# A fourth fold for the odd columns of an FFT done by matrix multiplication, and inverse tiles run one ahead

## Chip, cores, metric

One core of one Trainium2 chip. The metric is device time in microseconds (us) of one execution. TensorE (PE in the profile) multiplies, VectorE (DVE) and ScalarE (ACT) do elementwise work and copies, GpSimd (POOL) here mostly issues stores. The "granted clock" is the share of TensorE's full clock that the profile shows as granted, 1.00 being all of it. A run is "fast" when it is not over 1.5% above the fastest run of the same kernel; all comparisons below are between fast runs, except where a single look is named as such.

## The reference, cut to what matters

```python
def f(A_x, A_w_r, A_w_i, B_w1, B_b1, B_w2, B_b2, gate_w, B_x):      # S=2048, D=1024, F=3584, bf16
    x = A_x
    g = sigmoid((x * gate_w).sum(-1, keepdims=True))
    a = irfft2(rfft2(x) * (w_r + 1j * w_i))                         # spectral branch
    b = relu(B_x @ w1 + b1)**2 @ w2 + b2                            # MLP branch
    return g * a + (1 - g) * b
out, vjp = jax.vjp(f, ...);  return (out, *vjp(grad_out))           # forward and all gradients
```

## The kernel before

The transforms along D = 1024 and part of S are matmuls with small constant tables in fp16. Symmetry of cosine and sine is used by "folds": VectorE forms sums and differences of an entry and its mirror image, which halves the tables. A tile of 128 rows passes a row stage (eight matmuls of 128 columns into PSUM tile `pk`, copied by ScalarE to `ft`) and a column stage (eight matmuls into `pu`: four for the even columns, four for the odd). There are 16 forward tiles of x, 16 forward tiles of the gradient, and 32 inverse tiles. Names: P = 128, Q = 256, H = 512; T = 0 is x, T = 1 the gradient; `V` is VectorE's tensor_tensor; `fps` is a PSUM pool in which row and column stages share two buffers.

```python
def first_columns(fb, cf, T, i, ft, earlier=None):                   # forward
    pu = fps.tile([P, 2, H], FP32, name="pu", tag="ps2", bufs=2)
    column_stage(FWD, pu, ft, cf, earlier)
    u = fb.tile([P, D], FDT, name="u", tag="u", bufs=2)
    nc.scalar.copy(out=u[:].rearrange("p (h b r) -> p b h r", h=2, b=2),
                   in_=pu[:].rearrange("p b (h r) -> p b h r", h=2))
    st(out=z_scr[T]..., in_=u[:])

FWD = (  # (bank, first column, columns, skip, start/stop)
    (0, 0, 2*P, 0, 1), (0, 0, P+1, 0, 2), (0, 2*P, P, 0, 3), (0, 3*P, P, 0, 3),     # even
    (1, 0, 2*P, P, 1), (1, 0, 2*P, P, 2), (1, P, 2*P, P, 1), (1, P, 2*P, P, 2),     # odd: 4 x 256
)

# inverse, for each T and tile i:
    r = ...; ld(out=r, in_=y_scr...)
    pk = ...; eight matmuls (128 columns) from r;  rt = ...; nc.scalar.copy(out=rt[:], in_=pk[:])
    yield                                     # other work's matmuls are put in here
    pu = ...; column_stage(INV, pu, rt, ci)   # the same tile's
    nc.scalar.copy(out=e[:], in_=pu[:])
    ...                                       # VectorE: ev, tt, yo; store
    yield 2

# the first ~100 us, in program order (cut):
for i0 in range(0, NT, 4):
    gate(i0)                                  # scales four dbn tiles, VectorE
    next(stage, None)                         # stage: row or column stage of the next x tile
    for k in (i0 // 2, i0 // 2 + 1):
        turned(dbT, k, ..., nc.vector.tensor_copy)   # PE transposes into pt, VectorE copies to dbT
        next(stage, None)
    for k in (i0 // 2 + 2, i0 // 2 + 3):
        x_pair(k)                             # PE transposes, ScalarE copies to xT
        next(stage, None)
    ...
```

## Time and profile before

| | before |
|---|---|
| time, median of 4 runs (lowest to highest) | 1342.63 us (1342.42 to 1343.85) |
| PE busy | 98% of 1340.5 us |
| forward stages of x beside the first MLP matmuls | up to about 100 us |
| forward stages of the gradient | from 134 us, in a stretch (134 to 352 us) with PE busy for 216.79 of 218 us |
| inverse stages | 815 to 924 us (x), 924 to 1141 us (gradient) |

The page's busy shares, the three slices of the first 100 us and the rows of the column stages are in the prediction below. Columns: length, then busy us (count) of PE, weight loads, DVE, ACT, POOL, granted clock, DMA share, GB/s.

```profile
15.00:85.00 70.00, 65.49 (x711) 45.57 (x719) 67.61 (x143) 53.94 (x107) 13.93 (x21) 1.00 0.59 201
```
VectorE is busy for 67.61 of 70 us, 97%: more than PE, which has 4.5 us free here. And of PE's waits in the first 134 us (instruction, what it waits for: us in total, times, longest), this one will grow:

```profile
PE pt L543 <- DVE dbT L544: 2.0, 3, 1.0
```

### The profile page before, as it was taken

How to read it: one execution, taken by the hardware profiler on the slowest of the kernel's cores; microseconds unless marked ns; L12 is line 12 of the kernel's file. 1: busy time of each engine (PE TensorE's matmuls, PEld its weight loads, DVE VectorE, ACT ScalarE, POOL GpSimd, SP SyncE). 2: the span in 40 equal slices, each digit the busy share in tenths (PEclk: the TensorE clock that was granted, in tenths of full speed). 3: DMA queues.
4: the chain of work that ended last, by engine and by line, in shares of the span. 5: the costliest groups of instructions: out<-in, count | busy, mean ns of one | idle time of the engine just before them, and what ended most of it. 6: DMA issues, size and time to landing. Idle time of an engine off the chain costs nothing. (4 is left out here: it accounts for less than half of the span.)

```text
span 1340.5 us, 18698 instructions
## 1 busy us (share of the span) xinstructions
PE 1311.1 (98%) x6974; PEld 638.2 (48%) x7082; DVE 802.1 (60%) x1541; ACT 419.9 (31%) x658; POOL 295.7 (22%) x484
## 2 busy tenths in 40 slices
PE   7999999999999999999999999999999999999998
PEld 5654444444444444444444445455444444444443
DVE  7966767666665695677666772233655676742232
ACT  6854555555433323332333333343101111000000
POOL 0222223222222343434432222111000000000000
PEclk9999999999999999999999999999999999999999
DMA  8558778787778988888877558677878854753530
GB/s 285 186 178 253 253 235 258 241 254 236 215 236 247 270 248 188 222 177 230 222 179 181 128 164 265 216 229 231 207 194 225 253 168 134 210 166 95 151 103 24
DMA packets 217093, 273.30 MB, mean 204 GB/s; under 512 B 16989, under 2 KB 152171, under 8 KB 217003
## 3 DMA queue, kind: packets, MB, share of 16 engines
q1 hardware_dynamic: 181306, 153.84, 43.5%
q0 software_dynamic: 35696, 118.27, 27.3%
q8 instruction: 55, 0.90, 0.3%
q14 instruction: 36, 0.29, 0.1%
HBM read 147.25 MB, written 118.51 MB: 198 GB/s over the span
## 5 line engine op out<-in xcount | busy, mean ns | idle before, releaser
L619 PE MATMUL ph<-xT,w1g 128*128 128x512 bf16 x866 | 214.5, 381 | 2.9 <-ACT rT L621 1.2
L629 PE MATMUL pd<-dbT,w2T 128*128 128x512 bf16 x879 | 210.6, 379 | 2.5 <-DVE w2T L651 0.7
L840 PE MATMUL pw<-grd,res 128*128 128x512 bf16 x896 | 201.7, 379 | 0.0
L823 PE MATMUL pw<-dbn,grp 128*128 128x512 bf16 x875 | 199.9, 379 | 1.2 <-issue 0.2
L906 PE MATMUL acc<-w,hblk 128*128 128x512 bf16 x874 | 196.3, 379 | 1.2
L948 PE MATMUL accg<-w1Tr,hblk 128*128 128x512 bf16 x878 | 192.8, 379 | 0.9
L948 PEld LDWEIGHTS <-hblk 128*128 128x128 bf16 x896 | 87.6, 98 | 106.1 <-issue 0.9
L629 PEld LDWEIGHTS <-w2T 128*128 128x128 bf16 x896 | 87.3, 98 | 104.6 <-issue 1.4
L823 PEld LDWEIGHTS <-grp 128*128 128x128 bf16 x896 | 86.8, 98 | 103.0 <-issue 0.9
L906 PEld LDWEIGHTS <-hblk 128*128 128x128 bf16 x896 | 87.1, 98 | 99.4
L619 PEld LDWEIGHTS <-w1g 128*128 128x128 bf16 x896 | 87.0, 98 | 99.2 <-issue 2.8
L840 PEld LDWEIGHTS <-res 128*128 128x128 bf16 x896 | 86.5, 98 | 99.3 <-issue 1.1
L621 ACT ACTIVATE rT<-ph,b1col 128x512 bf16<-128x512 f32 x112 | 77.0, 687 | 144.9 <-PE ph L619 135.1
L633 DVE SCALAR_TENSOR_TENSOR dhT<-pd,rT 128x512 bf16<-128x512 f32 x112 | 75.2, 671 | 65.4 <-PE pd L629 57.3
L953 DVE TENSOR_TENSOR gxo<-accg,g 128x512 bf16<-128x512 f32 x32 | 22.1, 691 | 107.0 <-PE accg L948 103.5
L738 DVE STREAM_TRANSPOSE stg<-h2T 128x512 int32<-128x512 int32 x56 | 39.8, 711 | 73.7 <-ACT h2T L622 73.7
L827 ACT CAST wo<-pw 128x512 bf16<-128x512 f32 x56 | 32.8, 585 | 143.1 <-PE pw L823 132.2
L835 POOL DMA_DIRECT2D out_dram<-wo x112 | 56.0, 506 | 92.1 <-ACT wo L827 75.4
L498 DVE TENSOR_TENSOR ev<-e 128x256 f16<-128x256 f16 x32 | 9.2, 289 | 111.4 <-ACT e L495 111.4
L845 ACT CAST wo<-pw 128x512 bf16<-128x512 f32 x56 | 32.8, 587 | 127.2 <-PE pw L840 117.6
L490 ACT CAST rt<-pki 128x1024 f16<-128x1024 f32 x32 | 32.4, 1014 | 126.2 <-PE pki L488 126.0
L622 ACT ACTIVATE h2T<-rT 128x512 bf16<-128x512 bf16 x112 | 70.6, 630 | 3.1
(174 smaller groups left out, 1509.8 us busy)
## 6 DMA issues: line engine op xcount, KB each, us to landing
h2T_scr<-h2T POOLq DMA_DIRECT2D x28, 512.0 KB, 4.3
h_scr<-stg POOLq DMA_DIRECT2D x28, 512.0 KB, 6.9
dhT_scr<-dhT POOLq DMA_DIRECT2D x28, 512.0 KB, 8.0
dh_scr<-stgd POOLq DMA_DIRECT2D x28, 512.0 KB, 6.9
grp<-h_scr SPq DMA_DIRECT2D x112, 128.0 KB
grd<-dh_scr SPq DMA_DIRECT2D x112, 128.0 KB
hblk<-h2T_scr SPq DMA_DIRECT2D x8, 1792.0 KB
hblk<-dhT_scr SPq DMA_DIRECT2D x8, 1792.0 KB
```

Of the source, the lines that this page charges most:

```text
L619: mm(ph[:], lhsT=w1g[:, dc, fc % 2 * P : (fc % 2 + 1) * P], rhs=xT[:, dc, ss], start=(dc == 0), stop=(dc == DC - 1))
L621: nc.scalar.activation(rT[:], ph[:], ACT.Relu, bias=b1col[:, fc : fc + 1])
L622: nc.scalar.activation(h2T, rT[:], ACT.Square)
L629: mm(pd[:], lhsT=w_[:, ec // 2, ec % 2 :: 2], rhs=dbT[:, ec, ss], start=(ec == 0), stop=(ec == DC - 1),)
L633: return STT(out=dhT, in0=pd[:], scalar=2.0, in1=rT[:], op0=ALU.mult, op1=ALU.mult, accum_out=gb1part[:, fc, sb : sb + 1],)
L738: nc.vector.transpose(out=stg[:, :, c, :], in_=h2T[:, c, :].bitcast(I32).rearrange("p (b i) -> p b i", i=32))
L823: mm(pw[:], lhsT=cur[:, t // 2, 2 * fb_ * P + t % 2 : 2 * (fb_ + 1) * P : 2], rhs=dbn[:, t, hf * H : (hf + 1) * H], start=(t == 0), stop=( ...
L827: last = nc.scalar.copy(out=wo[:, hf * H : (hf + 1) * H], in_=pw[:])
L835: st(out=dst[q], in_=wo[32 * q : 32 * (q + 1), :])
L840: mm(pw[:], lhsT=xr[t][:, d_ * P : (d_ + 1) * P], rhs=cur[:, t], start=(t == 0), stop=(t == NT - 1),)
L906: mm(acc[:], lhsT=cur[:, fc, t2::2], rhs=w2[:, fc, cs], start=(fc == 0), stop=(fc == FC - 1))
L948: mm(acc[:], lhsT=cur[:, fc, t2::2], rhs=w1T[:, fc, 2 * hf : 2 * hf + 2, :], start=(fc == 0), stop=(fc == FC - 1),)
```

## The change

Intent: the odd columns have one more symmetry, between column l and D/2 - l. If sums and differences of such pairs are formed, each of the odd bank's four matmuls needs 128 columns in place of 256. In the forward stage VectorE forms them after the matmuls (from a new tile `w`), in the inverse before them (tile `rf`). Second, the inverse loop is reordered so that the rows of tile n are issued before the columns of tile n-1. The core of the diff (constant tables, row order and unchanged lines of the inverse cut):

```diff
     def first_columns(fb, cf, T, i, ft, earlier=None):
-        column_stage(FWD, pu, ft, cf, earlier)
+        column_stage(pu, ft, cf, earlier)
         u = fb.tile([P, D], FDT, name="u", tag="u", bufs=2)
-        nc.scalar.copy(out=u[:].rearrange("p (h b r) -> p b h r", h=2, b=2), in_=pu[:].rearrange(...))
+        w = fb.tile([P, 2, 2, 2, P // 2], FDT, name="w", tag="w", bufs=2)
+        nc.scalar.copy(out=w[:].rearrange("p c x g i -> p (c x g i)"), in_=pu[:, 1, :])
+        nc.scalar.copy(out=u[:].rearrange("p (h b r) -> p b h r", h=2, b=2)[:, 0], in_=pu[:, 0, :]...)
+        X, Y = (w[:, :, x].rearrange("p c g i -> p g c i") for x in range(2))
+        V(out=uv[:, 1::2, :, 0 : P // 2], in0=X, in1=Y, op=ALU.add)
+        V(out=uv[:, 3::-2, :, P - 1 : P // 2 - 1 : -1], in0=X, in1=Y, op=ALU.subtract)
...
-        (1, 0, 2 * P, P, 1), (1, 0, 2 * P, P, 2), (1, P, 2 * P, P, 1), (1, P, 2 * P, P, 2),
+        (1, 0, P, 3), (1, P, P, 3), (1, 2 * P, P, 3), (1, 3 * P, P, 3),
...
+        def folded(n):
+            fold[n] = fb.tile([P, 2, 2, P], FDT, name="rf", tag="rf", bufs=2)
+            rv = r[n][:].rearrange("p (c l) -> p c l", c=2)
+            a, b = rv[:, :, 1:Q:2], rv[:, :, H - 1 : Q : -2]
+            V(out=fold[n][:, 0], in0=a, in1=b, op=ALU.add)
+            V(out=fold[n][:, 1], in0=a, in1=b, op=ALU.subtract)
...
-            nc.scalar.copy(out=e[:], in_=pu[:])
+            nc.scalar.copy(out=e[:, 0, :], in_=pu[:, 0, :])
+            nc.scalar.copy(out=e[:, 1, :]..., in_=pu[:, 1, :]...)
...
+        load(0), load(1)
+        folded(0)
+        for n in range(len(tiles) + 1):
+            if n < len(tiles):
+                rows_back(n)
+                yield
+            if n > 0:
+                columns_back(n - 1)
+            if n + 2 < len(tiles):
+                load(n + 2)
+            if n + 1 < len(tiles):
+                folded(n + 1)
+            yield
```

More of the change, by code (lines that the diff above doesn't have):

```diff
@@ L65, in build_consts @@
     l4, l42 = np.arange(0, D // 2 + 1, 4), np.arange(2, D // 2, 4)
-    lo = np.concatenate([np.arange(1, D // 2, 4), np.arange(3, D // 2, 4)])
-    d0, d1 = np.arange(P), np.arange(P, 2 * P)
-    dz, dh = d0.copy(), d0.copy()
-    dz[0], dh[0] = Q, P
+    lo = np.concatenate([np.arange(1, Q, 4), np.arange(3, Q, 4)])
+    d0, dO = np.arange(P), np.arange(1, Q, 2)
+    dh, dz = d0.copy(), 2 * d0
+    dh[0], dz[0] = P, Q
     blk_n = np.concatenate([np.zeros((P, P + 1)), -np.sin(w(l4[1:-1], d0))], axis=1)
@@ L73, in build_consts @@
         blk_n, np.cos(w(l4, d0)), np.cos(w(l42, d0)), -np.sin(w(l42, dh)),
-        np.cos(w(lo, d0)), np.cos(w(lo, d1)), -np.sin(w(lo, dz)), -np.sin(w(lo, d1)),
+        np.cos(w(lo, 2 * d0)), np.cos(w(lo, dO)), -np.sin(w(lo, dO)), -np.sin(w(lo, dz)),
     ]
@@ L79, in build_consts @@
     cof = lambda l: np.where((l == 0) | (l == 2 * Q), 1.0, 2.0)[:, None]
-    dq = np.arange(Q)
-    dzq = dq.copy()
-    dzq[0] = Q
     m4, m42 = np.arange(0, D // 2, 4), np.arange(2, D // 2, 4)
-    m1, m3 = np.arange(1, D // 2, 4), np.arange(3, D // 2, 4)
+    mo = np.arange(1, Q, 2)
     da = np.arange(P + 1)
@@ L90, in build_consts @@
         ev, cof(m4) * np.cos(v(m4, da)), 2.0 * np.cos(v(m42, d0)), -2.0 * np.sin(v(m42, dh)),
-        2.0 * np.cos(v(m1, dq)), 2.0 * np.cos(v(m3, dq)), -2.0 * np.sin(v(m1, dzq)), -2.0 * np.sin(v(m3, dzq)),
+        2.0 * np.cos(v(mo, 2 * d0)), 2.0 * np.cos(v(mo, dO)), -2.0 * np.sin(v(mo, dz)), -2.0 * np.sin(v(mo, dO)),
     ]
@@ L249, in row_stage @@
         pk = fps.tile([P, 8, P], FP32, name="pk", tag="ps2", bufs=2)
-        for b, (row, o) in enumerate(((5, P), (4, 0), (4, P), (5, 0), (3, 0), (3, P), (1, 0), (1, P))):
-            first_ = mm(pk[:, b, :], lhsT=f[:, row, o : o + P], rhs=kmat, start=True, stop=True)
+        even = [(row, slice(o, o + P)) for row, o in ((5, P), (4, 0), (4, P), (5, 0))]
+        odd = [(row, slice(o, Q, 2)) for row, o in ((3, 0), (3, 1), (1, 1), (1, 0))]
+        for b, (row, o) in enumerate(even + odd):
+            first_ = mm(pk[:, b, :], lhsT=f[:, row, o], rhs=kmat, start=True, stop=True)
             if b == 0:
@@ L259, in first_columns, with column_stage @@
         pu = fps.tile([P, 2, H], FP32, name="pu", tag="ps2", bufs=2)
-        column_stage(FWD, pu, ft, cf, earlier)
+        column_stage(pu, ft, cf, earlier)
         u = fb.tile([P, D], FDT, name="u", tag="u", bufs=2)
+        w = fb.tile([P, 2, 2, 2, P // 2], FDT, name="w", tag="w", bufs=2)
+        nc.scalar.copy(out=w[:].rearrange("p c x g i -> p (c x g i)"), in_=pu[:, 1, :])
         nc.scalar.copy(
-            out=u[:].rearrange("p (h b r) -> p b h r", h=2, b=2), in_=pu[:].rearrange("p b (h r) -> p b h r", h=2)
+            out=u[:].rearrange("p (h b r) -> p b h r", h=2, b=2)[:, 0], in_=pu[:, 0, :].rearrange("p (h r) -> p h r", h=2)
         )
+        uv = u[:].rearrange("p (g c i) -> p g c i", g=4, c=2)
+        X, Y = (w[:, :, x].rearrange("p c g i -> p g c i") for x in range(2))
+        V(out=uv[:, 1::2, :, 0 : P // 2], in0=X, in1=Y, op=ALU.add)
+        V(out=uv[:, 3::-2, :, P - 1 : P // 2 - 1 : -1], in0=X, in1=Y, op=ALU.subtract)
         st(out=z_scr[T][:].rearrange("c (p i) l -> i (c p) l", i=S2)[i], in_=u[:])
-    FWD = (
-        (0, 0, 2 * P, 0, 1), (0, 0, P + 1, 0, 2), (0, 2 * P, P, 0, 3), (0, 3 * P, P, 0, 3),
-        (1, 0, 2 * P, P, 1), (1, 0, 2 * P, P, 2), (1, P, 2 * P, P, 1), (1, P, 2 * P, P, 2),
-    )
-    INV = FWD[:4] + ((1, 0, Q, 0, 1), (1, 0, Q, 0, 2), (1, Q, Q, 0, 1), (1, Q, Q, 0, 2))
-    def column_stage(table, pu, ft, mat, earlier=None):
+    BLOCKS = (
+        (0, 0, 2 * P, 1), (0, 0, P + 1, 2), (0, 2 * P, P, 3), (0, 3 * P, P, 3),
+        (1, 0, P, 3), (1, P, P, 3), (1, 2 * P, P, 3), (1, 3 * P, P, 3),
+    )
+    def column_stage(pu, ft, mat, earlier=None):
         o = 0
-        for b, (bank, lo, n, skip, f_) in enumerate(table):
-            out = pu[:, bank, lo : lo + n]
-            if skip:
-                out = pu[:, bank, :].rearrange("p (h c i) -> p c h i", h=2, c=2)[:, lo // P]
+        for b, (bank, lo, n, f_) in enumerate(BLOCKS):
             first_ = mm(
-                out, lhsT=ft[:, b, :], rhs=mat[:, o : o + n],
+                pu[:, bank, lo : lo + n], lhsT=ft[:, b, :], rhs=mat[:, o : o + n],
                 start=bool(f_ & 1), stop=bool(f_ & 2), skip_group_check=True,
@@ L480, in fft_out @@
         ld(out=ci[:], in_=cten["ci"].ap())
-        for T in range(2):
-            for i in range(NT):
-                r = fb.tile([P, H, 2], FDT, name="r", tag="r", bufs=3)
-                ld(out=r[:].rearrange("p j b -> p (j b)"), in_=y_scr[T][:].rearrange("c (p i) l -> i (c p) l", i=S2)[i])
-                pk = fps.tile([P, 8, P], FP32, name="pki", tag="ps2", bufs=2)
-                rf = r[:].rearrange("p j b -> p (j b)")
-                for b, (im, l_) in enumerate(((1, 0), (0, 0), (0, 2), (1, 2), (0, 1), (0, 3), (1, 1), (1, 3))):
-                    mm(pk[:, b, :], lhsT=rf[:, im * H + l_ : (im + 1) * H : 4], rhs=ki[:], start=True, stop=True)
-                rt = fb.tile([P, 8, P], FDT, name="rt", tag="rt", bufs=2)
-                nc.scalar.copy(out=rt[:], in_=pk[:])
-                yield
-                pu = fps.tile([P, 2, H], FP32, name="pui", tag="ps2", bufs=2)
-                column_stage(INV, pu, rt, ci)
-                e = fb.tile([P, 2, H], FDT, name="e", tag="e", bufs=2)
-                nc.scalar.copy(out=e[:], in_=pu[:])
-                ev = fb.tile([P, 2, Q], FDT, name="ev", tag="ev", bufs=2)
-                A, B = (e[:, 0, o : o + Q].rearrange("p (c d) -> p c d", c=2) for o in (0, Q))
-                V(out=ev[:, :, 0:P], in0=A, in1=B, op=ALU.add)
-                evf = ev[:].rearrange("p c d -> p (c d)")
-                V(out=evf[:, Q:P:-1], in0=A[:, 0, :], in1=B[:, 0, :], op=ALU.subtract)
-                V(out=evf[:, 2 * Q - 1 : Q + P : -1], in0=B[:, 1, 1:], in1=A[:, 1, 1:], op=ALU.subtract)
-                nc.vector.tensor_copy(out=ev[:, :, P : P + 1], in_=e[:, 0, P::Q].rearrange("p (c o) -> p c o", o=1))
-                tt = fb.tile([P, 2, 2, Q], FDT, name="tt", tag="tt", bufs=2)
-                V(out=tt[:, 0].rearrange("p a b -> p (a b)"), in0=evf, in1=e[:, 1, :], op=ALU.add)
-                V(out=tt[:, 1].rearrange("p a b -> p (a b)"), in0=evf, in1=e[:, 1, :], op=ALU.subtract)
-                yo = fb.tile([P, D], FDT, name="yo", tag="yo", bufs=2)
-                yv = yo[:].rearrange("p (a l) -> p a l", a=2)
-                V(out=yv[:, :, 0:Q], in0=tt[:, :, 0, :], in1=tt[:, :, 1, :], op=ALU.add)
-                V(out=yv[:, ::-1, H - 1 : Q : -1], in0=tt[:, :, 0, 1:Q], in1=tt[:, :, 1, 1:Q], op=ALU.subtract)
-                nc.vector.tensor_copy(out=yo[:, 0::Q], in_=tt[:, :, :, 0].rearrange("p a b -> p (a b)"))
-                st(out=ax_scr[T][i][:], in_=yo[:])
-                if T == 0 and i % 2 == 1:
-                    fc = 2 * (i - 1)
-                    if fc < FC:
-                        ld(out=w2[:, fc : fc + 4, :], in_=B_w2[fc * P : (fc + 4) * P, :].rearrange("(q p) e -> p q e", p=P))
-                yield 2
@@ new lines, in fft_out, with load @@
+        tiles = [(T, i) for T in range(2) for i in range(NT)]
+        r, fold, rt = {}, {}, {}
+        def load(n):
+            T, i = tiles[n]
+            r[n] = fb.tile([P, D], FDT, name="r", tag="r", bufs=3)
+            ld(out=r[n][:], in_=y_scr[T][:].rearrange("c (p i) l -> i (c p) l", i=S2)[i])
+        def folded(n):
[4 more added lines that the diff above has]
+            V(out=fold[n][:, 1], in0=a, in1=b, op=ALU.subtract)
@@ new lines, in rows_back @@
+        def rows_back(n):
+            pk = fps.tile([P, 8, P], FP32, name="pki", tag="ps2", bufs=2)
+            even = [r[n][:, im * H + l_ : (im + 1) * H : 4] for im, l_ in ((1, 0), (0, 0), (0, 2), (1, 2))]
+            odd = [fold[n][:, sign, im] for sign, im in ((0, 0), (1, 0), (1, 1), (0, 1))]
+            for b, block in enumerate(even + odd):
+                mm(pk[:, b, :], lhsT=block, rhs=ki[:], start=True, stop=True)
+            rt[n] = fb.tile([P, 8, P], FDT, name="rt", tag="rt", bufs=2)
+            nc.scalar.copy(out=rt[n][:], in_=pk[:])
@@ new lines, in columns_back @@
+        def columns_back(n):
+            T, i = tiles[n]
+            pu = fps.tile([P, 2, H], FP32, name="pui", tag="ps2", bufs=2)
+            column_stage(pu, rt[n], ci)
+            e = fb.tile([P, 2, H], FDT, name="e", tag="e", bufs=2)
+            nc.scalar.copy(out=e[:, 0, :], in_=pu[:, 0, :])
+            nc.scalar.copy(
+                out=e[:, 1, :].rearrange("p (c d x) -> p c d x", c=2, x=2),
+                in_=pu[:, 1, :].rearrange("p (c x d) -> p c d x", c=2, x=2),
+            )
+            ev = fb.tile([P, 2, Q], FDT, name="ev", tag="ev", bufs=2)
+            A, B = (e[:, 0, o : o + Q].rearrange("p (c d) -> p c d", c=2) for o in (0, Q))
+            V(out=ev[:, :, 0:P], in0=A, in1=B, op=ALU.add)
+            evf = ev[:].rearrange("p c d -> p (c d)")
+            V(out=evf[:, Q:P:-1], in0=A[:, 0, :], in1=B[:, 0, :], op=ALU.subtract)
+            V(out=evf[:, 2 * Q - 1 : Q + P : -1], in0=B[:, 1, 1:], in1=A[:, 1, 1:], op=ALU.subtract)
+            nc.vector.tensor_copy(out=ev[:, :, P : P + 1], in_=e[:, 0, P::Q].rearrange("p (c o) -> p c o", o=1))
+            tt = fb.tile([P, 2, 2, Q], FDT, name="tt", tag="tt", bufs=2)
+            V(out=tt[:, 0].rearrange("p a b -> p (a b)"), in0=evf, in1=e[:, 1, :], op=ALU.add)
+            V(out=tt[:, 1].rearrange("p a b -> p (a b)"), in0=evf, in1=e[:, 1, :], op=ALU.subtract)
+            yo = fb.tile([P, D], FDT, name="yo", tag="yo", bufs=2)
+            yv = yo[:].rearrange("p (a l) -> p a l", a=2)
+            V(out=yv[:, :, 0:Q], in0=tt[:, :, 0, :], in1=tt[:, :, 1, :], op=ALU.add)
+            V(out=yv[:, ::-1, H - 1 : Q : -1], in0=tt[:, :, 0, 1:Q], in1=tt[:, :, 1, 1:Q], op=ALU.subtract)
+            nc.vector.tensor_copy(out=yo[:, 0::Q], in_=tt[:, :, :, 0].rearrange("p a b -> p (a b)"))
+            st(out=ax_scr[T][i][:], in_=yo[:])
+            if T == 0 and i % 2 == 1:
+                fc = 2 * (i - 1)
+                if fc < FC:
+                    ld(out=w2[:, fc : fc + 4, :], in_=B_w2[fc * P : (fc + 4) * P, :].rearrange("(q p) e -> p q e", p=P))
```

## The prediction

Its sum came to -14.2 + 3 - 2.5 = -13.7 us, 1328.9 us. Rival 1 is the records of 98 ns: a gain of 4 x (112.5 - 98) x 64 = 3.7 us, about 1339 us, and 0.68 us for a column stage. The 162 ns are 2 x 587 - 1012 ns, the 0.3 us of signalling is what the 1.32 us of the example leave beside the copy of 1.01 us, and the 1 to 1.5 us for an eviction are an estimate of that size.

> **What bounds the kernel now.** I read the page's busy shares and slices first, then the busy time by stretch, then the groups by shape, then the timeline of the matrix engine around the two column stages, and last which waits hold that engine.
>
> From the page (busy us, share of the span; below it busy tenths in 40 slices of 33.5 us):
> ```profile
> PE 1311.1 (98%) x6974; PEld 638.2 (48%) x7082; DVE 802.1 (60%) x1541; ACT 419.9 (31%) x658; POOL 295.7 (22%) x484
> ...
> PE   7999999999999999999999999999999999999998
> ...
> DVE  7966767666665695677666772233655676742232
> ```
> TensorE (PE) is busy in nearly the whole span of 1340.5 us and the granted clock is full in every slice, so a microsecond of matmul taken out should be a microsecond off the end, except where something else already decides PE's pace. The only slice in which VectorE (DVE) also shows 9 is the second one. The stretches of the span (length, PE, weight loads, DVE, ACT, POOL busy, clock, DMA share, GB/s) say the same in microseconds:
> ```profile
> 0.00:33.50 33.50, 26.01 (x280) 18.68 (x284) 24.23 (x63) 22.99 (x47) 2.01 (x7) 1.00 0.82 285
> 33.50:67.00 33.50, 32.50 (x358) 23.02 (x362) 31.72 (x64) 27.49 (x52) 7.28 (x11) 1.00 0.56 187
> 67.00:100.00 33.00, 30.36 (x228) 16.97 (x229) 22.72 (x49) 18.62 (x33) 8.12 (x13) 1.00 0.52 179
> ```
> Those first 100 us are where the forward stages of x run: DVE has only 1.8 us free between 33.5 and 67 us. From 815 us to 924 us, where the first half of the inverse stages runs, DVE is busy for 33.6 of 109 us, and ACT for 45.0: plenty of room.
>
> A busy figure of PE is not its throughput, because one record lasts longer than the distance to the next one. So for the price of the column stage I use distances between starts in the timeline (start us, duration of the merged run, engine, line, what, count):
> ```profile
> 896.15 0.91 PE L281 MATMUL pui<-ci,rt 128*128 128x256 f16 x8
> 896.89 1.89 PE L840 MATMUL pw<-grd,res 128*128 128x512 bf16 x8
> 898.62 0.61 PE L488 MATMUL pki<-ki,r 128*128 128x128 f16 x8
> 899.07 3.62 PE L840 MATMUL pw<-grd,res 128*128 128x512 bf16 x16
> ```
> The eight matmuls of one inverse column stage take 896.89 - 896.15 = 0.74 us; the eight of a row stage, each of 128 columns, 899.07 - 898.62 = 0.45 us, or 56 ns each; the eight of 512 columns between them 1.73 us, or 216 ns each. Between those two a matmul costs (216 - 56)/(512 - 128) = 0.417 ns a column and about 3 ns, which makes 109 ns for 256 columns; single records in the column stages start 112 to 113 ns apart.
>
> [...]the row stage loads weights for each of its matmuls and still starts one every 56 ns, although a load's own record lasts 98 to 113 ns. [...](424 ns for 510 elements with a reversed operand, 424 ns for 512 without, both below); no tensor_tensor of fp16 with step 2 runs in the kernel before, and the new inverse fold has one. [...]the trace's copies of 512 columns (587 ns) and of 1024 (1012 ns) leave 162 ns.
>
> The rows (busy us, mean ns; idle us before them and its releasers):
> ```profile
> L281 PE MATMUL pu<-cf,ft 128*128 128x256 f16 x160 | 28.5, 274 | 0.1
> L281 PE MATMUL pui<-ci,rt 128*128 128x256 f16 x160 | 28.5, 274 | 4.5 <-ACT rt L490 3.8
> ...
> L845 ACT CAST wo<-pw 128x512 bf16<-128x512 f32 x56 | 32.8, 587 | 127.2 <-PE pw L840 117.6 <-issue 4.8 <-DMA out_dram<-wo 4.7
> L495 ACT CAST e<-pui 128x1024 f16<-128x1024 f32 x32 | 32.4, 1012 | 73.6 <-DVE ot L907 40.3 <-PE pui L281 27.2 <-issue 5.2
> ...
> L508 DVE TENSOR_TENSOR yo<-tt 128x512 f16<-128x512 f16 x32 | 13.6, 424 | 7.5 <-DMA ax_scr<-yo 6.9
> L509 DVE TENSOR_TENSOR yo<-tt 128x510 f16<-128x510 f16 x32 | 13.6, 424 | 0.0
> ...
> L498 DVE TENSOR_TENSOR ev<-e 128x256 f16<-128x256 f16 x32 | 9.2, 289 | 111.4 <-ACT e L495 111.4
> ```
>
> **The change, part by part.**
>
> *Removed from PE.* There are 32 forward and 32 inverse column stages. In each the odd bank's four matmuls go from 256 to 128 columns; their count, the even bank's four and all row stages keep their sizes. 4 x (112.5 - 57) = 222 ns per stage, so 64 x 0.222 = 14.2 us. All of it lies on the engine that sets the end. The new column stage should take about 0.74 - 0.22 = 0.52 us. This alone is 1.06% of 1342.6.
>
> *Added to DVE, forward.* Two tensor_tensor of 256 fp16 elements a tile. Records of this size last 289 ns and follow each other at some 0.20 us in the timeline; the new ones have inner runs of 64 with step 1 or -1, so I take 0.20 to 0.3 us. For the 16 tiles of x, 16 x 2 x 0.2 to 0.3 = 6.4 to 9.6 us come into the first 100 us. About a third of them fall into the stretch with 1.8 us of DVE to spare, so 1 to 2 us of it must push out what PE waits for (dbT, w2T, the folds). Elsewhere in the stage [...]PE waits for it now and then. I charge 3 us as a loss, a judgement; PE itself gives back 16 x 0.222 = 3.6 us there. So the early part is about even. The 16 tiles of the gradient run in the stretch from 134 us, where DVE has a third of the time free: no charge.
>
> *Added to DVE, inverse.* Two tensor_tensor of 256 elements with step 2, [...]in stretches where it is not the bound. No charge by itself.
>
> *Split of the PSUM copy.* One ACT copy of 1024 columns becomes two of 512: 2 x 587 - 1012 = 162 ns more, 64 x 0.162 = 10.4 us of ACT, on an engine with 69% free. It holds the PSUM pair 0.16 us longer.
>
> *Moved: one tile ahead.* Before, the column stage of a tile needs the copy of its own row stage. In the order of instructions the two stand only 5 to 7 long matmuls (1.1 to 1.5 us) apart in many places, and next to each other twice in the last part, while the copy takes 1.0 us and some 0.3 us of signalling. Example:
> ```profile
> 1028.34 0.61 PE L488 MATMUL pki<-ki,r 128*128 128x128 f16 x8
> 1030.11 0.91 PE L281 MATMUL pui<-ci,rt 128*128 128x256 f16 x8 [1.16 <-ACT rt L490]
> ```
> 1.77 us from start to start instead of 0.45: 1.32 us lost. Taking in every inverse column stage the start distance in front of it less the cost of the matmul there, 17 of 32 have such a hole, 7.2 us in sum (the row's 4.5 us of idle leaves out the draining end of the record before). In the changed kernel the row copy has a whole row stage's distance, so most of these go. But in the built order the new kernel also has places where row and column stages of two or three tiles stand close together (twice in the last part, thrice in the first), and they share two PSUM buffers, so some must wait for an eviction: 1 to 1.5 us each. I give 4.7 us of new holes: a net gain of 2.5 us.
>
> *Transfers.* Both constant tables shrink from 1665 to 1153 columns; not on the path. The w2 loads come one tile later, but the last one was issued 32 us before its first use. Still hidden.
>
> Sum: -14.2 + 3 - 2.5 = -13.7 us, 1328.9.
>
> **Rivals.**
> 1. *Weight loads take over:* a 128-column matmul cannot go below its load. [...]at 98 ns 3.7 us[...]. For: [...]the 98 ns records. Against: the row stage's 56 ns, even with its strided loads of 113 ns. Unlikely.
> 2. *DVE and ACT become the bound in the first 100 us:* all 10 us of new DVE work turn into PE waits. Then 1336. For: slice two. Against: slices one, three and four, with a third free.
> 3. *PSUM ping-pong:* bunched stages and the longer eviction cost more than the run-ahead saves, say 5 us net: 1336. For: two buffers only, and ACT's copies in the last part already wait for DVE (40.3 us "<-DVE ot"). Against: most stages of the new order alternate strictly, one between each 16 or 28 long matmuls.
> 4. *The holes nearly all go and the early part loses nothing:* 1342.6 - 14.2 - 7.2, about 1321.
>
> **Range and chances.** Rivals 2 to 4 give the edges: 1321 to 1336. Faster by over 2% needs under 1315.8, 27 us, more than all matmul savings plus all holes (21.4 us): 3%. Slower by over 2% needs PE to wait 40 us more: 1%.
>
> **What would show each step.** The distance from start to start over a column stage: 0.52 us (right), 0.6 or more (rival 1). The busy time by stretch before 100 us: the x stages should end at about the same time as before; 5 us later is rival 2. The waits for "rt" should vanish and holes at inverse stages sum to some 5 us; over 10 is rival 3. [...]The prediction is wrong if the early part reorders itself into something quite different, because a third of all PE idle lies there and the instruction order in it changes most.

## The result, and the profile after

The changed kernel takes 1337.7 us (median of 4 fast runs, 1336.4 to 1338.12), against 1342.63 us before. The ratio is 0.996, 95% interval 0.9942 to 0.9977; here and below a ratio is the mean time of one kernel's fast runs over that of the other's of the same rounds, so it isn't quite the ratio of the medians. A gain of 0.4%: within 2%, as expected, but 8.8 us slower than the 1328.9 us foretold and above the upper end of the range, 1336.

The page of the changed kernel (busy us; slices in tenths):

```profile
PE 1298.0 (97%) x6974; PEld 630.2 (47%) x7082; DVE 836.0 (63%) x1669; ACT 424.5 (32%) x722; POOL 295.7 (22%) x484
...
PE   7889999999999999999999999999999899999998
...
DVE  6986777676666596785667863434756776842232
```
PE's busy time fell by 13 us, but the span by only 5.9 us (1340.5 to 1334.6 in the profiled runs). The second and third digits of PE went from 9 to 8. The same three stretches as in the prediction show it for the changed kernel, and after them stands the window from 15 to 85 us:

```profile
0.00:33.50 33.50, 23.87 (x238) 16.81 (x241) 22.31 (x58) 20.97 (x42) 1.47 (x6) 1.00 0.80 274
33.50:67.00 33.50, 29.90 (x370) 21.77 (x373) 32.47 (x78) 28.99 (x58) 7.21 (x11) 1.00 0.56 186
67.00:100.00 33.00, 28.02 (x231) 16.12 (x234) 26.62 (x65) 20.08 (x46) 7.93 (x12) 0.95 0.48 162
```
```profile
15.00:85.00 70.00, 59.42 (x666) 41.23 (x673) 66.41 (x155) 53.12 (x112) 12.13 (x19) 0.98 0.57 195
```
From 15 to 85 us PE is busy for 6 us less and has also *done* less (666 matmul records against 711), while VectorE is nearly as full as before (66.41 us, 95%).

To place the 5.9 us I cut both traces at the same points of the work, by the first weight load of a stage; below, this table is called the ledger. "x" reaches from the first MLP matmul's load to the 129th load of that kind.

| stretch | before | after | difference | foretold |
|---|---|---|---|---|
| start, to the first MLP matmul | 9.13 | 9.66 | +0.5 | 0 |
| x: forward stages of x | 104.02 | 108.84 | +4.8 | -0.6 |
| forward stages of the gradient | 350.68 | 347.74 | -2.9 | -3.6 |
| weight gradients, spectral middle | 353.68 | 352.88 | -0.8 | 0 |
| inverse, first half | 106.44 | 101.80 | -4.6 | } -9.6 |
| inverse, second half | 217.06 | 213.75 | -3.3 | } |
| rest | 199.49 | 199.97 | +0.5 | 0 |
| sum | 1340.5 | 1334.6 | -5.9 | -13.7 |

(The foretold column divides the prediction's -14.2 of matmuls by the number of tiles: 3.55, 3.55 and 7.1, adds its +3 to x and its -2.5 to the inverse.) One border does not cut the same work: in the changed kernel the last inverse column stage comes at 1140.76 us, after the first load of the rest, which starts at 1134.66; before, it comes ahead of that load. So 0.52 us of inverse work is counted under "rest" there: the rest is unchanged, and the inverse gave 7.4 us, not 7.9.

What the column stage costs, in the timeline of PE (start, duration of the merged run, engine, line, what, count):

```profile
822.38 0.68 PE L283 MATMUL pui<-ci,rt 128*128 128x256 f16 x8
822.90 3.61 PE L875 MATMUL pw<-grd,res 128*128 128x512 bf16 x16
```
0.52 us from start to start, where it was 0.74. Over all column stages after 120 us the median is 0.523 us forward and 0.522 us inverse; single odd matmuls start 59 ns apart. The groups (busy us, mean ns, idle before and its releasers):

```profile
L496 DVE TENSOR_TENSOR rf<-r 128x256 f16<-128x256 f16 x32 | 13.4, 420 | 22.6 <-DMA r<-y_scr 14.1 <-PE pki L504 8.6
L271 DVE TENSOR_TENSOR u<-w 128x256 f16<-128x256 f16 x32 | 9.1, 283 | 0.0
L270 DVE TENSOR_TENSOR u<-w 128x256 f16<-128x256 f16 x32 | 8.7, 272 | 7.7 <-DMA z_scr<-u 4.4 <-ACT w L263 3.1
L514 ACT CAST e<-pui 128x512 f16<-128x512 f32 x32 | 19.1, 597 | 0.0
L283 PE MATMUL pui<-ci,rt 128*128 128x256 f16 x32 | 8.7, 273 | 1.5 <-ACT e L514 1.0 <-ACT rt L506 0.5
```
The step-2 fold of the inverse takes 420 ns, the forward adds 272 and 283 ns. The wait of the inverse column stages for `rt`, 3.8 us before, is 0.5 us now; in its place come other small ones. PE's waits of the first 134 us:

```profile
PE pt L578 <- DVE dbT L579: 7.6, 9, 1.8
...
PE pd L664 <- DVE dhT L668: 1.5, 1, 1.5
```
The transposes `pt` now wait 7.6 us for VectorE's copies `dbT`, where they waited 2.0 us. How an add of 0.2 us does that, the timeline of VectorE shows:

```profile
75.90 1.22 DVE L579 COPY dbT<-pt 128x1024 bf16<-128x1024 bf16 x1
77.23 0.29 DVE L270 TENSOR_TENSOR u<-w 128x256 f16<-128x256 f16 x1
77.44 0.28 DVE L271 TENSOR_TENSOR u<-w 128x256 f16<-128x256 f16 x1
77.64 0.42 DVE L234 TENSOR_TENSOR f<-uv 128x510 f16<-128x510 f16 x1
77.98 0.42 DVE L235 TENSOR_TENSOR f<-uv 128x510 f16<-128x510 f16 x1
78.31 1.22 DVE L579 COPY dbT<-pt 128x1024 bf16<-128x1024 bf16 x1
```
and that of PE beside it (in brackets the idle time and what ended it):

```profile
77.18 0.61 PE L578 MATMUL pt<-identb,dbn 128*128 128x128 bf16 x8 [0.88 <-DVE dbT L579]
79.58 0.61 PE L578 MATMUL pt<-identb,dbn 128*128 128x128 bf16 x8 [1.80 <-DVE dbT L579]
```
In this timeline VectorE takes these instructions one after the other: none starts over 0.09 us before or 0.11 us after the end of the one ahead of it. Between two `dbT` copies stand the two adds (0.41 us from the first's start to what follows) and two folds (0.67 us), and PE, which has two PSUM buffers for its transposes, waits 1.80 us until the second copy is through. Right after these two waits the clock is lowered:

```profile
80.00:85.00 5.00, 4.74 (x29) 2.46 (x28) 4.28 (x9) 2.57 (x6) 0.54 (x1) 0.66 0.12 43
```
The granted clock is 0.66 over these 5 us (0.50 from 82 to 84 us), where before it is 1.00 in the same window. At full clock the same work would take 0.34 x 5 = 1.7 us less, an estimate. It isn't a chance of this one run: the mean granted clock over the whole span is 0.997 to 0.998 in all four runs of the changed kernel, and 0.998 to 1.0 in the 35 runs of the kernel before beside the experiments, with 0.998 in four of them. The traces of e6 and e18, which have the same x tiles, show a lowered clock between 70 and 90 us too (mean over the whole span 0.993 to 0.997 in their eight runs).

### The profile page after: what moved, and what is told of

The parts are those of the page before. It is cut to its first block, busy times and chain, and to the rows that moved or that the text cites. A ratio compares the mean times of both kernels' runs of the same rounds, so it can differ in the third digit from the quotient of the medians.

```text
span 1334.6 us, 18965 instructions
## 1 busy us (share of the span) xinstructions
PE 1298.0 (97%) x6974; PEld 630.2 (47%) x7082; DVE 836.0 (63%) x1669; ACT 424.5 (32%) x722; POOL 295.7 (22%) x484
## 4 chain that ended last, share of the span: by engine, by line
PE 83%; DVE 9%; DMA 3%; issue 2%; ACT 1%; POOL 1%; SPq 0%; DVEq 0%; ACTq 0%; POOLq 0%
PE accg L983 14%; PE acc L941 14%; PE pw L875 14%; PE ph L654 13%; PE pd L664 13%; PE pw L858 7%; DMA out_dram<-wo 2%; DVE dbacc L835 1%; PE pui L283 1%; DVE dbT L579 1%; PE pki L504 1%; PE pk L250 1%; DVE x L332 1%; PE pu L283 1%; DVE t L451 1%
## 5 line engine op out<-in xcount | busy, mean ns | idle before, releaser
L664 PEld LDWEIGHTS <-w2T 128*128 128x128 bf16 x896 | 87.6, 98 | 107.8 <-issue 5.6
L780 DVE STREAM_TRANSPOSE stgd<-dhT 128x1024 bf16<-128x1024 bf16 x56 | 69.3, 1240 | 1.2
L332 DVE TENSOR_TENSOR x<-px,common 128x1024 f16<-128x1024 f32 x32 | 38.8, 1220 | 45.3 <-ACT common L329 45.3
```

The lines of the kernel that those rows point to most:

```text
L332: V(out=x[:, j, :, 0:H].rearrange("p c (i g) -> p c i g", g=4), in0=px[:].rearrange("p c (g i) -> p c i g", g=4), in1=common[:].rearrange( ...
L664: mm(pd[:], lhsT=w_[:, ec // 2, ec % 2 :: 2], rhs=dbT[:, ec, ss], start=(ec == 0), stop=(ec == DC - 1),)
L780: nc.vector.transpose(out=stg[:, :, :, c, :].rearrange("p b k i -> p k b i"), in_=dhT[:, c, :].rearrange("p (k b i) -> p k b i", b=4, i=32),)
```

## The experiments

Theory at the start: in the x stretch VectorE sets the pace; the adds delay it, and the shorter matmuls give nothing back there. Rivals: the split PSUM copy does it; the new instruction order does it; or the loss arises in the inverse. "x" is the x stretch of the single profiled run; identical forward programs (before, e1, e4, e14) spread from 104.0 to 105.2 us in it, and the two with the whole changed forward, after and e6, from 107.8 to 108.8, so less than 1.2 us isn't read as an effect.

| label | what it is | result | median us | ratio to before [95%] | x us |
|---|---|---|---|---|---|
| (after) | the change | right | 1337.70 | 0.9960 [0.9942, 0.9977] | 108.84 |
| e1_x_old | after, x tiles' forward as before | right | 1332.07 | 0.9924 [0.9909, 0.9939] | 104.04 |
| e2_x_no_adds | after, no adds for x | wrong | 1333.04 | 0.9929 [0.9914, 0.9944] | 104.09 |
| e3_before_adds | before, with two adds per x tile | wrong | 1349.48 | 1.0047 [1.0030, 1.0064] | 108.98 |
| e4_inverse_only | only the inverse part of the change | right | 1335.73 | 0.9947 [0.9932, 0.9962] | 105.19 |
| e5_x_pool | after, x adds on GpSimd | right | 1338.69 | 0.9975 [0.9949, 1.0000] | 111.30 |
| e6_not_ahead | after, inverse not one ahead | right | 1344.61 | 1.0013 [0.9997, 1.0029] | 107.78 |
| e8_scale_pool | e1, scaling of dbn on GpSimd | right | 1358.31 | 1.0114 [1.0097, 1.0131] | 129.63 |
| e9_short_only | before, x odd matmuls 128 wide | wrong | 1344.08 (3 fast) | 1.0005 [0.9986, 1.0024] | - |
| e9b_short_look | the same again, one look | wrong on purpose | 1345.94 | single run | 105.19 |
| e10_split_copy | before, x copy split, one look | right | 1343.43 | single run | 104.77 |
| e11_dbt_act | after, 4 of 16 dbT copies on ScalarE | right | 1335.32 | 0.9955 [0.9927, 0.9983] | 106.59 |
| e12_x_old_dbt_act | e1 with the same | right | 1331.69 | 0.9918 [0.9902, 0.9934] | 104.67 |
| e13_no_adds_dbt_act | e2 with the same | wrong | 1341.56 | 0.9990 [0.9972, 1.0009] | 112.64 |
| e14_ahead_only | before, inverse one ahead | right | 1339.90 | 0.9978 [0.9957, 1.0000] | 105.18 |
| e15_before_u4 | before, four u buffers | right | 1342.64 | 1.0007 [0.9992, 1.0022] | 105.93 |
| e16_short_u4 | e9, four u buffers | wrong | 1345.29 | 1.0027 [1.0012, 1.0042] | 108.70 |
| e17_x_old_u4 | e1, four u buffers | right | 1334.17 | 0.9945 [0.9928, 0.9961] | 106.78 |
| e18_after_u4 | after, four u buffers | right | 1339.09 | 0.9978 [0.9963, 0.9993] | 109.47 |

The kernel before had medians of 1341.9 to 1343.1 us in all these sessions.

A lowered clock is part of some of these x stretches. Summed over windows of 10 us, length times what is missing to full clock, it makes an estimated 1.7 us in after, e6, e9b, e15 and e17, 3.4 us in e5, e13 and e18, 5.1 us in e16 and about 10 us in e8; in before, e1 to e4, e10 to e12 and e14 the clock is full there.

### Which part costs the time

**e1: the x tiles' forward as before, all else new.**

```diff
-                ft[i] = row_stage(f1, folds(f1, xs[i]), kf[:])
+                ft[i] = row_stage_x(f1, folds(f1, xs[i]), kf[:])        # before's row order
...
-                first_columns(f1, cf, 0, i - 1, ft[i - 1])
+                first_columns_x(f1, cf, 0, i - 1, ft[i - 1])            # before's columns, one copy, no adds
...
+    ld(out=cf[:, 5 * P + 1 : 9 * P + 1], in_=cten["cg"].ap())           # new table's odd part for the gradient
```

> Only the 16 forward tiles of x go back to the old column stage (256-column matmuls, one copy, no adds); the gradient's tiles and the inverse keep the change. Theory A (new adds crowd VectorE in the first 100 us, PE waits for what stands behind them): the loss of some 9 us goes, the x tiles' 3.6 us of matmul saving goes too: about 1331 us, 7 us faster than the changed kernel, and the gradient phase starts no later than in the kernel before. Rival C (the loss is not in the x tiles): about 1341.

1332.07 us, 0.9924: 5.6 us faster than the full change (1337.7 - 1332.07), though 16 x 0.222 = 3.6 us of matmul came back. The x stretch is 104.04 us, as before. So the forward part for x is a loss as a whole.

**e2: the change without the adds for x** (wrong result: ScalarE writes the odd columns straight into `u`).

```diff
-        nc.scalar.copy(out=w[:]..., in_=pu[:, 1, :])
+        nc.scalar.copy(out=w[:]... if T else uv[:, 1::2], in_=pu[:, 1, :] if T else pu[:, 1, :].rearrange(...))
...
+        if T:                                   # adds for the gradient alone
             V(out=uv[:, 1::2, ...], in0=X, in1=Y, op=ALU.add)
             V(out=uv[:, 3::-2, ...], in0=X, in1=Y, op=ALU.subtract)
```

> The changed kernel without the two adds per x tile (wrong result on purpose); short matmuls, split copy and the new order of stages stay. Theory A: 1337.7 less the loss of 8 to 9 us, about 1329; the long waits for dbT copies fall from 7.6 us to about 2, no half-clock stretch. Rival B (the split copy or the reordered row and column stages cost it): 1336 to 1338.

1333.04 us, x 104.09 us. With the short matmuls, the split copy and the new instruction order, but without the adds, the stretch is as long as with the old forward (e1, 104.04 us). So the adds cost 108.84 - 104.09 = 4.75 us (4.7 us by the medians, 1337.7 - 1333.04; 3.7 us with e6's 107.78 in after's place), and the shorter matmuls bring nothing that shows. That is less than the 8 to 9 us expected, which had counted on the matmuls' gain. Some 1.7 of the 4.75 us come by way of the lowered clock, which e2 has nowhere in its first 120 us. The waits confirm that the saved PE time is still spent as idle time:

```profile
PE pt L579 <- DVE dbT L580: 4.8, 9, 1.0
```

**e3: before, with two adds of the same shapes per x tile** (wrong: they overwrite `u` from `ft`).

```diff
+        if T == 0:
+            X, Y = (ft[:, 4 * x : 4 * x + 4, 0 : P // 2].rearrange("p (g c) i -> p g c i", c=2) for x in range(2))
+            V(out=uq[:, 1::2, :, 0 : P // 2], in0=X, in1=Y, op=ALU.add)
+            V(out=uq[:, 3::-2, :, P - 1 : P // 2 - 1 : -1], in0=X, in1=Y, op=ALU.subtract)
```

> The kernel before, with two adds of the same size and shape put on VectorE for each x tile (wrong result on purpose), matmuls and copies unchanged. Theory A: 6 to 9 us slower than the kernel before, 1349 to 1352, all of it before 100 us. Rival B: within 2 us of 1342.6.

1349.48 us, x 108.98 us: 5.0 us more than before (by the medians of the whole kernel 6.9), with the old matmuls and the old copy, and at full clock in all of the first 120 us. The cost is the adds' own. At the 0.41 us a pair of the timeline above, their queue time is 16 x 0.41 = 6.6 us; three quarters of it reach the end. (The adds also stand between the copy and the store of `u`; e3 doesn't separate that from VectorE's time.)

**e4: only the inverse part** (both forward stages as before).

```diff
-    (row_stage, first_columns and the odd part of table cf of the change)
+    (those of before)
```

> Forward stages all as before, inverse changed. By the sum: 32 x 0.222 = 7.1 us of matmul and 1 to 2 us of holes: about 1334. If the inverse gives less than 6 us (over 1336.6), a second part of the forecast was wrong too. The difference from the run with only the x tiles old is the gradient's 3.6 us.

1335.73 us, 0.9947: 7.1 us gained. e1, which has the gradient's forward part as well, gains 10.2 us (0.0076 x 1342.6). The difference, 3.1 us, agrees with the 2.9 us of the ledger for the gradient.

**e9 and e9b: before, with the x tiles' odd matmuls cut to 128 columns and nothing else** (wrong).

```diff
-        column_stage(FWD, pu, ft, cf, earlier)
+        column_stage(SHORT if T == 0 else FWD, pu, ft, cf, earlier)
...
+    SHORT = FWD[:4] + ((1, 0, P, 0, 3), (1, P, P, 0, 3), (1, 2 * P, P, 0, 3), (1, 3 * P, P, 0, 3))
```

> The kernel before, with only the odd matmuls of the 16 x tiles cut from 256 to 128 columns (wrong result on purpose); one copy, no adds. If PE sets the pace in the first 100 us, as the forecast had it: 16 x 0.222 = 3.6 us faster, 1339.0. If PE only follows VectorE's copies there, as the run without adds suggests: within 1 us of the kernel before, 1342.

> The short-matmul kernel again for its profile alone, as the first profile fell into a run three times as long. From the first long matmul to the 128th weight load of the same group the kernel before takes 104.0 us. If PE only follows there: 103.5 to 104.5; if PE sets the pace: 100.5.

Three fast runs of e9 give a ratio of 1.0005 [0.9986, 1.0024]: taking 3.6 us of matmul out of this stretch brings nothing that shows; the interval allows some 2 us. (Two of the three, at a mean clock of 1.0, took 1344.08 and 1340.96 us, the third, at 0.997, 1345.19.) Its profiled run took 3942.99 us in a slow state in which the matmuls of 512 columns took 834 to 1047 ns (379 to 381 before) and the weight loads 173 to 215 ns (98 before); I have no explanation for it and don't use it, and took one more look, e9b (1345.94 us, state unknown because it is alone). In it the x stretch is 105.19 us, with the clock lowered for a while (granted 0.89 and 0.94 from 50 to 70 us), and the freed time shows as a wait for VectorE, 5.2 us where before it was 2.0:

```profile
PE pt L544 <- DVE dbT L545: 5.2, 9, 1.0
```

**e10: before, with the x tiles' PSUM copy split in two.**

```diff
-        nc.scalar.copy(out=uh, in_=ph_)
+        for b_ in (1, 0):
+            nc.scalar.copy(out=uh[:, b_], in_=ph_[:, b_])               # T == 0
```

> The kernel before with the x tiles' copy out of PSUM split in two (right result), one look. 16 x 0.16 us on ScalarE: same stretch 104.0 us in the kernel before; within 1 us of it if the split costs nothing, 106 or more if it explains part of the loss.

1343.43 us in one look, x 104.77 us: within the spread of identical programs. One look would be little, but e2 has the split copy too and 104.09 us: it isn't the cause.

### Can the cost be moved to another engine?

**e5: the x tiles' adds on GpSimd.**

```diff
+        add_ = V if T else nc.gpsimd.tensor_tensor
-        V(out=uv[:, 1::2, ...], in0=X, in1=Y, op=ALU.add)              # and the subtract
+        add_(out=uv[:, 1::2, ...], in0=X, in1=Y, op=ALU.add)
```

> The changed kernel with the two adds of each x tile on GpSimd in place of VectorE (right result). If only VectorE's time is short there: like the run without these adds, about 1333. If [...]its slower adds hold the buffers that the stores read: 1335 to 1340.

1338.69 us, 0.9975, x 111.30 us: no gain over the change. The groups of GpSimd:

```profile
L272 POOL TENSOR_TENSOR u<-w 128x256 f16<-128x256 f16 x16 | 11.8, 740 | 0.0
...
L271 POOL TENSOR_TENSOR u<-w 128x256 f16<-128x256 f16 x16 | 10.8, 676 | 48.7 <-ACT w L263 44.1 <-DMA z_scr<-u 4.6
```
An add is about 2.5 times as long as on VectorE (676 and 740 against 272 and 283 ns), and GpSimd also issues the stores in this part. So relieving VectorE of them isn't a clean test of the theory: the load went, but a longer way to `u` took its place.

**e8: e1, with the scaling of the gradient tiles `dbn` on GpSimd**, meant to give VectorE room.

```diff
-            nc.vector.tensor_scalar(out=dbn[:, i, :], in0=dbn[:, i, :], scalar1=omg[:, i : i + 1], ...)
+            nc.gpsimd.tensor_scalar(out=dbn[:, i, :], in0=dbn[:, i, :], scalar1=omg[:, i : i + 1], ...)
```

> The kernel with only the x tiles old (1332.1), and the 16 scalings of the gradient rows (489 ns each on VectorE, 7 us of distance in all) moved to GpSimd. If VectorE's time sets the pace of the first 100 us, taking 7 us off it should give 2 to 5 us: 1327 to 1330. If GpSimd's scalings are slow, transposes wait for them instead and it is no faster: 1332 to 1340.

A miss: 1358.31 us, 26 us slower than e1. GpSimd needs 2869 ns for what VectorE does in 489 ns, and the transposes now wait for it (group, then PE's wait):

```profile
L654 POOL TENSOR_SCALAR dbn<-dbn,omg 128x1024 bf16<-128x1024 bf16 x16 | 45.7, 2869 | 16.5 <-DMA dbn<-in_grad_out_dram 12.6 <-ACT gcol L652 3.8
```
```profile
PE pt L624 <- POOL dbn L654: 16.6, 10, 2.4
```

**e11, e12, e13: a quarter of the dbT copies on ScalarE**, in the change, in e1 and in e2.

```diff
-            turned(dbT, k, lambda i: dbn[:, i, :], of_tile, nc.vector.tensor_copy)
+            turned(dbT, k, ..., <first half VectorE, second half ScalarE> if k % 2 else nc.vector.tensor_copy)
```

> The changed kernel with 4 of the 16 copies of the transposed gradient (1.22 us each on VectorE) given to ScalarE. If VectorE's time sets the pace of the first 100 us: 4.9 us off it gives 2 to 4 us, about 1335, and the waits of transposes for VectorE's copies fall from 7.6 us. If ScalarE is as short there (21 to 29 of 33.5 us busy): no faster, 1337 to 1340.

> The kernel with only the x tiles old (1332.1) with the same 4 copies on ScalarE. If VectorE's time sets the pace there even without the adds: 1329 to 1331, the fastest of all. If it doesn't: 1332 to 1334.

> The changed kernel without the x tiles' adds (wrong result on purpose, 1333.0) and with the 4 copies of the transposed gradient on ScalarE. Three engines stand near full use in the x stretch. If VectorE was what kept the shorter matmuls from paying, taking 4.9 us off it must now free them: the stretch of 104.0 us falls to 100 to 102, the time to 1329 to 1331. If something else (ScalarE, the order, the loads) holds it: 104, 1333.

e11's x stretch is 106.59 us, 2.2 us below the change's. Its clock is full there, so 1.7 of the 2.2 us may be the lowered clock that stayed away; that VectorE's queue was bought back in part is likely, not shown. Its runs spread from 1333.37 to 1339.88 us, and its ratio can't be told from the change's. e12 is the fastest kernel here, 1331.69 us, but its interval overlaps e1's, and its x stretch of 104.67 us is not below e1's. e13 (wrong) came out worse, 1341.56 us: a single wait of 6.6 us stands in its trace,

```profile
PE pd L665 <- DVE dhT L669: 6.6, 1, 6.6
```
because VectorE's `dhT` stood in its queue behind `stg`, which waited 6.3 us for the load of `w2r`. In these two runs relieving VectorE did not bring the stretch below 104 us.

**e15 to e18: four buffers for u in place of two.** The chain in this stretch goes on from VectorE to a store: the copy into `u` waits 3.5 us for an earlier store of `u` on ScalarE before, and 4.4 us on VectorE after. Four buffers take that wait away (room is made by letting two w2 tiles share one set of buffers).

```diff
-        u = fb.tile([P, D], FDT, name="u", tag="u", bufs=2)
+        u = fb.tile([P, D], FDT, name="u", tag="u", bufs=4)
...
-            w2r = wb.tile([P, D], BF16, name="w2n", tag="w2n", bufs=2)
+            w2r = wb.tile([P, D], BF16, name="w2n", tag="w2r", bufs=4)
```

> The kernel before with four buffers in place of two for the forward result u (the room comes from two loads of w2 sharing a tag), so that no copy waits for the store of z (3.5 us in one wait near 90 us). If that store holds the end of the x stretch: 104.0 us there falls by 1 to 3 us, 1340 to 1342. If not: same time within 1 us.

> The kernel before with short x matmuls (wrong result on purpose) and four buffers of u. If the store is what kept the short matmuls from paying: 3 us or more faster than the kernel before with four buffers, about 1338. If VectorE's copies keep it: within 1 us of it.

> The kernel with only the x tiles old (1332.1), with four buffers of u. If the store holds the end of the x stretch: 1329.5 to 1331.5, the fastest; if not, 1332.

> The changed kernel with four buffers of u. There VectorE itself waited 4.4 us for the store. If that wait is a good part of the adds' cost of 4.8 us: 1334 to 1336; if the cost is VectorE's time alone: 1337 to 1338.5.

None is faster than its partner: the x stretches are 1.9, 3.5, 2.7 and 0.6 us longer. The wait for the store is gone, but VectorE's `stg` now waits for the load of `w2r` (0.2 us before, 2.1 us in e15, 3.3 us in e16), and PE then waits for `dhT`, 2.3 us in e15 and 3.5 us in e16. Against its partner each also has more lowered clock in the stretch, by the estimate above 1.7 us in e15, e17 and e18 and 3.4 us in e16, which is most or all of what they are longer. The edit also changes which buffers the w2 loads wait for, so it can't be said that the store's wait alone was worth nothing.

### What running one tile ahead is worth

**e14: before, with the inverse one tile ahead and nothing else.**

```diff
+        for n in range(len(tiles) + 1):
+            if n < len(tiles):
+                rows_back(*tiles[n]); yield
+            if n > 0:
+                columns_back(*tiles[n - 1])
+            yield
```

> The kernel before, with only the inverse stages run one tile ahead; no new fold, matmuls as before. The forecast saw the run-ahead as a cure for old holes of 7.2 us: 1336 to 1340. If its use is only to hide the new fold's adds, as the run without it suggests, it gives the old kernel little: 1341 to 1343.

1339.9 us, 0.9978: about 3 us, though the interval reaches from 0 to 6 us. In the ledger the two halves fall from 106.44 and 217.06 us to 103.13 and 216.32. PE's waits around the inverse stages: the column stages no longer wait for `rt` (3.8 us before), a row stage waits 0.8 us for the row copy that holds a PSUM buffer, and a new wait comes, for a load:

```profile
PE pki L489 <- DMA r<-y_scr: 1.8, 1, 1.8
```

**e6: the change, with the inverse not one ahead.**

```diff
-        for n in range(len(tiles) + 1):
-            if n < len(tiles): rows_back(n); yield
-            if n > 0: columns_back(n - 1)
+        for n in range(len(tiles)):
+            rows_back(n)
+            yield
+            columns_back(n)
```

> The changed kernel with the inverse stages not run one tile ahead: row stage and column stage of the same tile in turn, as before. The forecast gave the run-ahead a net 2.5 us; the traces of before and changed show under 1 us. By the forecast about 1340; by the traces 1338 to 1339, with more holes in front of the inverse column stages and as many fewer elsewhere.

1344.61 us, 7 us slower than the change, where 1338 to 1340 was expected. The halves are 103.14 and 221.41 us, in sum 9.0 us more than after's 101.80 and 213.75 (8.5 with the stage that after has behind the border), and even 1.1 us more than before's, though 7.1 us of matmul have gone. PE's waits there:

```profile
PE acc L939 <- DVE bGo L941: 4.4, 2, 3.5
PE pki L504 <- DVE rf L496: 3.8, 1, 3.8
```
PE waits once for the fold and twice for `bGo`, an eviction of the long matmuls by VectorE: 8.2 us that before has not; the changed kernel has 4.7 us of waits in this part. The clock is lowered after them as well (mean over the whole span 0.994, in after 0.998): the 28 long matmuls behind the one wait take 7.89 us and the 29 behind the other 8.57 us, where 28 take 6.21 us elsewhere, so that some 3.8 of the 8.5 us, an estimate, come by way of the clock. I read it as one queue in which the fold's two instructions of 420 ns and the evictions stand behind each other; the trace shows the waits, not that order of causes. So running ahead is worth about 3 us with the old fold and 7 us (by time) to 8.5 us (in the profile) with the new one.

## Why the prediction was wrong in size

**Steps that held.** The column stage went to 0.52 us as worked out, and 59 ns per matmul rule out the weight loads (rival 1), whose records last 98 ns. The step-2 fold takes 420 and 419 ns for 256 elements, where 256 without step 2 took 289 ns and 512 took 424; the author's estimate of its time is among the cuts. The split copy costs 588 + 597 - 1012 = 173 ns more, foretold 162. The gradient's forward part gave 2.9 of 3.55 us. The inverse gave its 7.1 us of matmul (7.4 us in all). The w2 loads stayed hidden, and the change stayed within 2%, as foretold.

**First failed step: "PE itself gives back 16 x 0.222 = 3.6 us there".** In the x stretch it gives back nothing: e9 removes these columns alone and has a ratio of 1.0005, and e2 against e1 shows 104.09 against 104.04 us. The freed time turns into waits for `dbT` (2.0 to 5.2 us in e9b). The prediction took its rule, "a microsecond of matmul taken out should be a microsecond off the end, except where something else already decides PE's pace", and then did not apply the exception in the one place where its own slice two called for it.

**Second failed step: "I charge 3 us as a loss, a judgement".** The adds cost 4.75 us (after less e2) or 5.0 us (e3): in the changed kernel partly as waits and partly as the lowered clock that follows them, in e3 without it. The estimate went wrong in the window: "about a third of them fall into the stretch with 1.8 us of DVE to spare" used thirds of 100 us, of which the first contains 15 us before the first column stage and the last the part after them. Over 15 to 85 us VectorE has 2.4 us free in all, and in the changed kernel thirteen of the sixteen tiles' adds lie in it. Together the first two steps are 5.4 us of the miss: -0.6 foretold, +4.8 found. This is rival 2, "all 10 us of new DVE work turn into PE waits. Then 1336", in a milder form, and the sign that the prediction gave for it ("5 us later is rival 2") came: the x stretch ends 5.3 us later, 118.50 against 113.15 us. About 5 us turned into lost time, but the 3.6 us of matmul were lost as well, which rival 2 had not counted.

**Third failed step: "a net gain of 2.5 us" from running ahead.** The inverse gave 7.4 us with the border put right, 0.3 beyond the matmuls. Holes around the inverse stages (start distances less the cost of the matmul, over 0.15 us each) fell only from 8.1 to 7.2 us in sum, where about 5 was foretold. The step weighed two things, gone `rt` waits against shared PSUM buffers, and left out the third: "no charge by itself" for the fold's adds. e14 shows that running ahead alone gives what was foretold (about 3 us), and e6 that the fold without it loses more than its matmuls bring. Running ahead paid for the adds; the little that is left over is the net gain.

**The balance.** x 5.4, inverse 2.2, gradient 0.6 us; start +0.5 and middle -0.8 are small and not explained. The sum is 7.9 us with rounding, from -13.7 to -5.9 us. By the medians of the times the change is -4.9 us.

**Open.** What holds the x stretch at 104 us. That VectorE does so in the kernel before is supported by 97% busy and by e3, but taking copies off it (e12) doesn't shorten it, and taking the store's wait away (e15 to e18) brings the w2 load forward as the next wait. Several things of nearly the same length stand behind each other there; no run separates them all. Nor is the slow run of e9 explained, nor shown why the clock falls where it does: in after and e6 it is seen after waits of PE, no more.

**A better version.** e1, which keeps the old forward for the x tiles, takes 1332.07 us, 0.8% below before and 0.4% below the change, with a right result; e12 (1331.69 us) can't be told from it.

## What to carry to other kernels

A fold that trades matmul columns for elementwise work paid here only where TensorE set the pace (2.9 of 3.55 us for the gradient, a loss of 4.8 us for x): ask for that stage's own window, from its first to its last instruction, before counting a saving, and apply the fold to those stages alone. Here a pair of instructions of 0.41 us delayed what stood behind it in VectorE's queue, so look for a copy that another engine waits for in the same queue; running a tile ahead can pay for such an addition (here it was worth about 3 us with the old fold, e14, and 7 us with the new one, e6), and should then not be counted as a gain of its own. When a change has two parts, price each without the other: here one hid the cost of the other.
